# The last 64 rows of two batches on the two column halves of TensorE, and one product of batch 0 on row halves again

## The chip, the core and the metric

The kernel runs on one core of one Trainium2 chip. The metric is device time in microseconds (us), from start to end of one execution. A core has a matrix engine (TensorE, PE in the profile, with its weight loads listed apart as PEld), VectorE (DVE), ScalarE (ACT), GpSimd (POOL) and SyncE (SP, here it only issues transfers). TensorE multiplies a stationary block (the weights, lhsT) of up to 128 x 128 by a moving block of up to 512 columns and writes the result to PSUM, from where VectorE or ScalarE takes it. The stationary block can be smaller: the array can work as two column halves (128 x 64), two row halves (64 x 128) or four quarters (64 x 64), each with weights of its own.

## What is computed

A linear attention over 8 batches, 8 heads, 576 rows and 64 values per head, followed by an MLP mixer:

```python
def phi(x): return np.where(x > 0, x, np.exp(x) - 1.0) + 1.0
q_p, k_p = phi(q), phi(k)
kv  = einsum('bhsd,bhse->bhde', k_p, v);  z = sum(k_p, axis=2)
x   = einsum('bhsd,bhde->bhse', q_p, kv) / (einsum('bhsd,bhd->bhs', q_p, z) + 1e-6)
# x as (batch, 576, 512)
h   = relu(x^T @ w_tok1) @ w_tok2          # over the 576 rows, through 256
u   = x + h^T
out = u + relu(u @ w_ch1) @ w_ch2          # over the 512 columns, through 1536
```

The 576 rows of a batch are four blocks of 128 and a tail of 64. The product with `w_tok2` is called mm2 in the kernel.

## The kernel before

The batches are taken in pairs. While TensorE does the large products of batch n (mm3 and mm4, with `w_ch1` and `w_ch2`), small steps of batch n + 1 are put between them at fixed places (`AT`). R is 4, the number of full row blocks, so block R is the tail. D is 64, DM is 512, NT is 2 (256 = 2 x 128), T is 9.

mm2 takes a list of row blocks. For the tail it multiplies the full 128-column weights, of which 64 columns belong to the tail, and uses one half of the 128 rows that result: the lower half for an even batch, the upper for an odd one. The tails of a pair meet in one tile `ut` of 128 rows, which is transposed and gives one extra block of the large products.

```python
half = [slice(0, 64), slice(64, 128)]

def w2v(kt, r, b=0):
    at = D * (T * kt + 2 * r - (b if r == R else 0))
    return w2p[:, at:at + 128]

def mm2(n, rs, add=False):
    b = n % 2
    ...                                   # ps: two banks of PSUM from the pool "sm"
    for i, r in enumerate(rs):
        for kt in range(NT):
            nc.tensor.matmul(out=ps[:, i], lhsT=w2v(kt, r, b),          # L261
                             rhs=ar[b][:, kt, :], start=(kt == 0),
                             stop=(kt == NT - 1 and not add))
    ...
    if rs[0] == R:
        h = half[b]
        nc.vector.tensor_tensor(out=ut[n // 2 % 2][h], in0=ps[h, 0],    # L269
                                in1=x[b][h, R], op=ALU.add)
    ...
```

The steps of a batch n > 1, and where they stand in the order of the large products:

```python
out_ += [("mm2a", lambda: mm2(n, [0, 1])), ("mm2b", lambda: mm2(n, [2, 3])),
         ("mm2t", lambda: mm2(n, [R]))]
out_ += [("uta", lambda: utr_dma(n, [0, 1])), ("utb", lambda: utr_dma(n, [2, 3]))]
if n % 2:
    out_.append(("utt", lambda: utr_tail_dma(n // 2)))     # transposes ut by a transfer
...
AT = {"kv": 0, "nd00": 2, ..., "mm1": 9, "mm2a": 11, "mm2b": 12, "mm2t": 14,
      "uta": 11, "utb": 12, "utt": 14}
```

Batch 0 is done apart, at the start, where everything waits for the first loads. phi(k) is kept as two terms, kr and kp, both multiplied with v0. c is a group of four heads:

```python
def kv_first(c, copy):
    ps = sm_tile()[:, :, 0:2 * D]
    for k_ in (kr, kp):
        for t in range(T):
            on, off = k_ is kr and t == 0, k_ is kp and t == T - 1
            if k_ is kr:                                   # row halves, 64 x 128
                for a in range(2):
                    nc.tensor.matmul(out=ps[:, a], lhsT=k_[half[a], c, t],       # L366
                                     rhs=v0[half[a], 2 * c:2 * c + 2, t], start=on, stop=off)
            else:                                          # quarters, 64 x 64
                for a, i in QUARTERS:
                    nc.tensor.matmul(out=ps[half[i], a, i * D:(i + 1) * D],      # L371
                                     lhsT=k_[half[a], c, t, i],
                                     rhs=v0[half[a], 2 * c + i, t], start=on, stop=off)
    for i in range(2):
        copy(out=kvbd[0][half[i], c, :, i * D1:(i + 1) * D1 - 1],                # L375
             in_=ps[half[i], :, i * D:(i + 1) * D])
```

On row halves, the blocks of two different heads are multiplied with each other too; the copy takes only the two blocks that are wanted. Two products of batch 0 already stand on column halves (`ps[half[e]]`): L439, whose matmuls alternate between the halves, and L447, batch 0's own tail on one half.

```python
for kt in range(NT):                                       # in mm2_first, columns cs
    for e in range(2):
        nc.tensor.matmul(out=ps[half[e], i], lhsT=w2r[:, kt, :, 2 * r + e],      # L439
                         rhs=ar[0][:, kt, cs], start=(kt == 0), stop=(kt == NT - 1))
...
for kt in range(NT):                                       # in mm2_first_tail
    nc.tensor.matmul(out=ps[half[0]], lhsT=w2r[:, kt, :, 2 * R], rhs=ar[0][:, kt],   # L447
                     start=(kt == 0), stop=(kt == NT - 1))
```

Of the kernel before, what the change touches and what calls it, by code (L numbers as in the profile page):

```python
# [9 lines left out]
FP32 = mybir.dt.float32  # L10
BF16 = mybir.dt.bfloat16
AF = mybir.ActivationFunctionType
ALU = mybir.AluOpType
# [5 lines left out]
def kernel(  # L19
# [20 lines left out]
    nc = tc.nc  # L40

    B, H, S, D = q.shape
    DM = H * D
    DTOK = moe_w_tok1.shape[1]
    DCH = moe_w_ch1.shape[1]
    R = 4
    R1 = R + 1
    T = 2 * R + 1
# [3 lines left out]
    NT = DTOK // 128  # L52
# [10 lines left out]
    ps_sm = ctx.enter_context(tc.tile_pool(name="ps_sm", bufs=2, space=bass.MemoryType.PSUM))  # L63

    def const(name, shape, dt=BF16):
        return consts.tile(shape, dt, name=name, tag=name)
# [4 lines left out]
    w2p = const("w2p", [128, (NT * T + 1) * D])  # L71
# [6 lines left out]
    kr = const("kr", [128, 2, T, 2, D])  # L78
# [4 lines left out]
    x = [const(f"x{b}", [128, R1, DM]) for b in range(2)]  # L83
    ar = [const(f"ar{b}", [128, NT, DM]) for b in range(2)]
    u = [const(f"u{b}", [128, R, DM]) for b in range(2)]
    ut = [const(f"ut{i}", [128, DM]) for i in range(2)]
# [10 lines left out]
    half = [slice(0, 64), slice(64, 128)]  # L97
# [56 lines left out]
    def bank():  # L154
        return ps_big.tile([128, 512], FP32, name="bank", tag="big")
# [6 lines left out]
    def kv(n, cs):  # L162
        b = n % 2
        ps = ps_sm.tile([128, 2, 512], FP32, name="kv_ps", tag="sm")[:, :, 0:2 * D1].rearrange(
            "p a (c e) -> p a c e", c=2)
        for c in cs:
            for t in range(T):
                for a, i in QUARTERS:
                    nc.tensor.matmul(out=ps[half[i], a, c], lhsT=kp[half[a], c, t, i],  # L169
                                     rhs=vs[half[a], 2 * c + i, t],  # L170
                                     start=(t == 0), stop=(t == T - 1))
        cs = slice(cs[0], cs[-1] + 1)
        for i in range(2):
            at = slice(i * D1, (i + 1) * D1)
            nc.scalar.copy(out=kvbd[b][half[i], cs, :, at].transpose([0, 2, 1, 3]),
                           in_=ps[half[i], :, cs])
# [13 lines left out]
    def qtr(n, c, put=nc.scalar.copy):  # L190
        tp = ps_sm.tile([128, 2, 8, 128], BF16, name="tp", tag="sm")
        for h, ts in enumerate(TS):
            qtr_mm(c, ts, tp[:, h])
        for h, ts in enumerate(TS):
            qtr_put(n, c, ts, tp[:, h], put)
# [32 lines left out]
    def nd(n, g, rs):  # L228
        nd_mm(n, g, rs)
        nd_end(n, g, rs)  # L230
# [7 lines left out]
# [4 lines that stand above are left out]
    def mm1(n):  # L242
        b = n % 2
        ps = ps_sm.tile([128, NT, DM], FP32, name="a_ps", tag="sm")
        for mt in range(NT):
            ms = slice(128 * mt, 128 * mt + 128)
            for r in range(R1):
                nc.tensor.matmul(out=ps[:, mt], lhsT=w1t[:, b, ms] if r == R else w1[:, r, ms],  # L248
                                 rhs=x[b][:, r, :], start=(r == 0), stop=(r == R))
        for mt in range(NT):  # L250
            nc.scalar.activation(out=ar[b][:, mt, :], in_=ps[:, mt], func=AF.Relu)  # L251

    def mm2(n, rs, add=False):

        b = n % 2
        m = len(rs)
        ps = bank().rearrange("p (a d) -> p a d", a=1) if n == 1 else ps_sm.tile(
            [128, 2, DM], FP32, name="h_ps", tag="sm")
# [5 lines that stand above are left out]
            if add:  # L264
                nc.tensor.matmul(out=ps[:, i], lhsT=identity, rhs=x[b][:, r, :], start=False,
                                 stop=True)
        if rs[0] == R:
            h = half[b]
            nc.vector.tensor_tensor(out=ut[n // 2 % 2][h], in0=ps[h, 0], in1=x[b][h, R], op=ALU.add)  # L269
        elif add:  # L270
            nc.scalar.copy(out=u[b][:, rs[0]:rs[0] + m], in_=ps[:, 0:m])
        else:
            nc.vector.tensor_tensor(out=u[b][:, rs[0]:rs[0] + m], in0=ps[:, 0:m],  # L273
                                    in1=x[b][:, rs[0]:rs[0] + m], op=ALU.add)

    def mm2_half(n, c):
        b = n % 2
        cs = COLS[c]
        for rs in ([0, 1], [2, 3]):
            ps = ps_sm.tile([128, 2, 512], FP32, name="h_ps", tag="sm")[:, 0].rearrange(  # L280
                "p (r c) -> p r c", r=2)
            add = rs[0] == 0
            for i, r in enumerate(rs):
                if add:
                    nc.tensor.matmul(out=ps[:, i], lhsT=identity, rhs=x[b][:, r, cs],
                                     start=True, stop=False)
                for kt in range(NT):
                    nc.tensor.matmul(out=ps[:, i], lhsT=w2v(kt, r), rhs=ar[b][:, kt, cs],
                                     start=(kt == 0 and not add), stop=(kt == NT - 1))
            if add:  # L290
                nc.scalar.copy(out=u[b][:, 0:2, cs], in_=ps)
            else:
                nc.vector.tensor_tensor(out=u[b][:, 2:4, cs], in0=ps, in1=x[b][:, 2:4, cs],
                                        op=ALU.add)
# [22 lines left out]
    def sm_tile():  # L317
        return ps_sm.tile([128, 2, 512], FP32, name="bank2", tag="sm")
# [39 lines left out]
    def kv_first(c, copy):  # L358

        ps = sm_tile()[:, :, 0:2 * D]  # L360
        for k_ in (kr, kp):
            for t in range(T):
                on, off = k_ is kr and t == 0, k_ is kp and t == T - 1
                if k_ is kr:
                    for a in range(2):
                        nc.tensor.matmul(out=ps[:, a], lhsT=k_[half[a], c, t],  # L366
                                         rhs=v0[half[a], 2 * c:2 * c + 2, t],
                                         start=on, stop=off)
                else:
# [7 lines that stand above are left out]
# [95 lines left out]
    def utr_dma(n, rs):  # L472
        b = n % 2
        nc.sync.dma_start_transpose(
            out=uT[b][:, rs[0]:rs[0] + len(rs)].rearrange("p r j c -> p (r j) c"),
            in_=u[b][:, rs[0]:rs[0] + len(rs)].rearrange("p r d -> p (r d)"))

    def utr_tail_dma(p):
        nc.sync.dma_start_transpose(out=uTt, in_=ut[p % 2])
# [204 lines left out]
    def steps(n):  # L684

        out_ = [("kv", lambda: kv(n, range(2)))]
        if n == 1:
            puts = [nc.scalar.copy, nc.vector.tensor_copy if n == 1 else nc.scalar.copy]
            out_ += [(f"qt{c}", lambda c=c: qtr(n, c, puts[c])) for c in range(2)]
        for i, rs in enumerate(([0, 1], [2, 3], [4])):  # L690
            for g in range(2):
                out_.append((f"nd{i}{g}", lambda g=g, rs=rs: nd(n, g, rs)))
        out_.append(("mm1", lambda: mm1(n)))
        if n > 1:
            out_ += [("mm2a", lambda: mm2(n, [0, 1])), ("mm2b", lambda: mm2(n, [2, 3])),
                     ("mm2t", lambda: mm2(n, [R]))]
            out_ += [("uta", lambda: utr_dma(n, [0, 1])), ("utb", lambda: utr_dma(n, [2, 3]))]
            if n % 2:
                out_.append(("utt", lambda: utr_tail_dma(n // 2)))
        return out_  # L700
# [36 lines left out]
    for nm, fn in first[1:2] + late + first[2:3] + first[0:1] + first[3:]:  # L737
        fill += [(at0[nm], fn)]
    fill += [(23, fn) for fn in (
        lambda: mm4_end(0, 0), lambda: mm4_end(0, 1), lambda: mm2_half(1, 0),  # L740
        lambda: mm4_end(0, 2), lambda: mm2_half(1, 1), lambda: utr(1, [0]),
        lambda: mm2(1, [R]), lambda: utr(1, [1]), lambda: mm4_end(0, 3))]
    run(big, sorted(fill, key=lambda e: e[0]))
# [20 lines left out]
    for n in range(2, B):  # L764
        p, b = divmod(n, 2)
# [48 lines left out]
```

## Time and profile before

| | |
|---|---|
| device time, median of 3 | 264.82 us (264.30 to 264.83) |
| span of the profiled execution | 263.1 us |
| busy, TensorE | 253.5 us (96%) |
| busy, VectorE | 158.7 us (60%) |
| busy, ScalarE | 133.2 us (51%) |
| busy, GpSimd | 33.3 us (13%) |

In a line of a group or of the timeline, `L261 PE MATMUL h_ps<-ar,w2p 128*128 128x512 bf16 x2` is: line 261 of the kernel, the engine, the operation, the tile written and the tiles read, the part of the array used (128*128 is all of it, 128*64 a column half, 64*128 a row half, 64*64 a quarter), partitions and columns of the moving block, its type, and how many in a row. In a timeline the two numbers ahead are the start and the time from the first start to the last end, both in us; `[0.42 <-issue]` is the idle time of the engine just ahead and what ended it. In a list of waits the numbers are the sum in us, the count and the longest. Matmuls are pipelined, so the time that one holds the engine is read from the distance between starts. A timeline over a narrow window shows only the instructions that run in it, so its first start and count fix single matmuls.

### The profile page before, as it was taken

To read this page: it belongs to the slowest core of one execution; us is meant where nothing else is said; L and a number is where in the kernel's file an instruction comes from. 1 tells how busy PE (TensorE), PEld (TensorE's weight loads), DVE (VectorE), ACT (ScalarE), POOL (GpSimd) and SP (SyncE) were. 2 spreads that over 40 slices of the span, in tenths; PEclk is the share of its full clock that TensorE was granted. 3 is DMA by queue.
4 is the path that set the end of the run, shared out by engine and by line. 5 is a ranking of instruction groups with operands and counts; after the bars stand their busy time and mean duration, and the time that the engine had idled before them with its cause. 6 is when DMAs were issued, how large, how long until landed. Compare 5 with 4: busy or idle time off the path is not lost.

```text
span 263.1 us, 5193 instructions
## 1 busy us (share of the span) xinstructions
PE 253.5 (96%) x2118; PEld 134.1 (51%) x2136; DVE 158.7 (60%) x313; ACT 133.2 (51%) x204; POOL 33.3 (13%) x54
## 2 busy tenths in 40 slices
PE   7699999999999999999999999999999999999994
PEld 3485455554744554445554554455554454444642
DVE  5755978966839696939684287939684272420122
ACT  4664887368364458435780368335870353027300
POOL 9630210110002300020001300030001300000000
PEclk9999999999999999999999999999999999999999
DMA  7999999599306995699999990771074500730043
GB/s 256 246 204 278 370 205 397 190 205 401 151 0 130 192 367 223 140 272 393 288 360 197 283 397 14 157 165 33 0 134 119 120 2 0 152 107 2 0 99 103
DMA packets 50088, 48.35 MB, mean 184 GB/s; under 512 B 30288, under 2 KB 35536, under 8 KB 50064
## 3 DMA queue, kind: packets, MB, share of 16 engines
q1 hardware_dynamic: 41904, 35.53, 45.7%
q0 software_dynamic: 7440, 11.44, 20.7%
q10 hardware_dynamic: 720, 1.05, 1.3%
q8 instruction: 17, 0.28, 0.4%
q14 instruction: 7, 0.06, 0.1%
HBM read 35.85 MB, written 9.44 MB: 172 GB/s over the span
## 4 chain that ended last, share of the span: by engine, by line
PE 90%; DMA 3%; ACT 2%; DVE 1%; POOL 1%; issue 1%; ACTq 0%; POOLq 0%
PE h_ps L516 33%; PE c_ps L490 32%; PE a_ps L248 5%; PE h_ps L261 5%; PE c_ps L504 4%; PE nd_ps L210 3%; DMA cr<-in_v_dram 3%; PE kv_ps L169 2%; PE h_ps L553 1%; PE bank L428 1%; POOL qT L597 1%; PE bank L439 1%; PE bank L393 1%; PE bank L366 0%; DVE u L441 0%
## 5 line engine op out<-in xcount | busy, mean ns | idle before, releaser
L497 ACT ACTIVATE cr<-c_ps 128x512 bf16<-128x512 f32 x91 | 53.4, 599 | 76.3 <-PE c_ps L490 76.2
L490 PE MATMUL c_ps<-uT,wc 128*128 128x512 bf16 x384 | 91.5, 379 | 0.0
L516 PE MATMUL h_ps<-wc,cr 128*128 128x512 bf16 x365 | 84.5, 379 | 0.5
L516 PEld LDWEIGHTS <-cr 128*128 128x128 bf16 x372 | 36.0, 98 | 41.6
L490 PEld LDWEIGHTS <-wc 128*128 128x128 bf16 x384 | 35.7, 98 | 36.4 <-issue 0.9
L533 DVE TENSOR_TENSOR o_sb<-h_ps,u 128x512 f32<-128x512 f32 x31 | 21.1, 689 | 23.1 <-PE h_ps L516 21.4
L538 POOL DMA_DIRECT2D out_dram<-o_sb x24 | 15.0, 629 | 151.9 <-DVE o_sb L533 151.9
L222 DVE TENSOR_TENSOR x<-nd_ps,den 128x512 bf16<-128x512 f32 (+1 forms) x42 | 25.3, 603 | 1.4
L139 DVE TENSOR_SCALAR e<-e 128x1152 bf16<-128x1152 bf16 x30 | 13.9, 464 | 12.6 <-ACT e L125 12.6
L273 DVE TENSOR_TENSOR u<-h_ps,x 128x1024 bf16<-128x1024 f32 x12 | 14.3, 1220 | 10.1 <-PE h_ps L261 10.1
L125 ACT ACTIVATE e<-k_raw 128x1152 bf16<-128x1152 f32 x16 | 18.7, 1169 | 2.3 <-DMA k_raw<-in_k_dram 2.3
L125 ACT ACTIVATE e<-q_raw 128x1152 bf16<-128x1152 f32 x16 | 18.5, 1160 | 2.3 <-DMA q_raw<-in_q_dram 2.3
L219 DVE TENSOR_SCALAR den<-nd_ps 128x8 f32<-128x8 f32 (+1 forms) x42 | 6.9, 164 | 17.9 <-PE nd_ps L210 17.2
L210 PEld LDWEIGHTS <-qT 128*128 128x128 bf16 x140 | 11.4, 98 | 9.3 <-issue 0.2
L261 PE MATMUL h_ps<-ar,w2p 128*128 128x512 bf16 x58 | 15.6, 379 | 0.1
L210 PE MATMUL nd_ps<-kvbd,qT 128*128 128x130 bf16 x140 | 15.1, 223 | 0.0
L248 PE MATMUL a_ps<-x,w 128*128 128x512 bf16 x50 | 13.9, 379 | 0.3
L543 DVE TENSOR_TENSOR o_sb<-h_ps,ut 128x512 f32<-128x512 f32 x4 | 2.8, 690 | 18.7 <-PE h_ps L516 18.7
L251 ACT ACTIVATE ar<-a_ps 128x512 bf16<-128x512 f32 x14 | 7.6, 594 | 12.7 <-PE a_ps L248 12.7
L151 ACT CAST vs<-v_raw 128x1152 bf16<-128x1152 f32 x12 | 13.9, 1159 | 0.0
L140 DVE TENSOR_TENSOR qp<-e,y 128x1152 bf16<-128x1152 bf16 x16 | 12.1, 759 | 0.6
L131 DVE TENSOR_SCALAR y<-q_raw 128x1152 bf16<-128x1152 f32 x16 | 12.1, 757 | 0.3
(107 smaller groups left out, 220.9 us busy)
## 6 DMA issues: line engine op xcount, KB each, us to landing
k_raw<-in_k_dram SPq DMA_DIRECT2D x16, 576.0 KB, 9.7
q_raw<-in_q_dram SPq DMA_DIRECT2D x16, 576.0 KB, 7.0
v_raw<-in_v_dram SPq DMA_DIRECT2D x14, 576.0 KB, 11.2
out_dram<-o_sb POOLq DMA_DIRECT2D x24, 256.0 KB, 4.4
wc<-in_moe_w_ch_dram POOLq DMA_DIRECT2D x8, 384.0 KB, 9.7
out_dram<-o_sb SPq DMA_DIRECT2D x9, 128.0 KB, 2.3
out_dram<-o_sb ACTq DMA_DIRECT2D x7, 128.0 KB, 2.6
out_dram<-o_sb POOLq DMA_DIRECT2D x6, 128.0 KB, 6.8
```

Of the source, the lines that this page charges most:

```text
L125: nc.scalar.activation(out=e, in_=f, func=AF.Exp)
L139: nc.vector.tensor_scalar(out=e, in0=e, scalar1=1.0, scalar2=None, op0=ALU.min)
L210: nc.tensor.matmul(out=o[:, a], lhsT=qT[b][:, t0:t0 + 128], rhs=kvbd[b][:, c, a], start=True, stop=True)
L222: nc.vector.tensor_tensor(out=x[b][:, rs[0]:rs[0] + m, HG * D * g:HG * D * (g + 1)].rearrange("p r (h d) -> p r h d", h=HG), in0=v_[:, :, ...
L248: nc.tensor.matmul(out=ps[:, mt], lhsT=w1t[:, b, ms] if r == R else w1[:, r, ms], rhs=x[b][:, r, :], start=(r == 0), stop=(r == R))
L261: nc.tensor.matmul(out=ps[:, i], lhsT=w2v(kt, r, b), rhs=ar[b][:, kt, :], start=(kt == 0), stop=(kt == NT - 1 and not add))
L273: nc.vector.tensor_tensor(out=u[b][:, rs[0]:rs[0] + m], in0=ps[:, 0:m], in1=x[b][:, rs[0]:rs[0] + m], op=ALU.add)
L490: nc.tensor.matmul(out=ps, lhsT=wc1[:, kj, 128 * mc:128 * mc + 128], rhs=uT[b][:, :, kj], start=(kj == 0), stop=(kj == NDM - 1))
L497: nc.scalar.activation(out=cr[b][:, mc, :], in_=ps, func=AF.Relu)
L516: nc.tensor.matmul(out=ps, lhsT=crt[:, kc, :] if t == 8 else cr[b][:, kc, 128 * r:128 * r + 128], rhs=wc2[:, kc, :], start=(kc == 0), stop ...
L533: nc.vector.tensor_tensor(out=o, in0=ps, in1=u[b][:, r, :], op=ALU.add)
L538: (nc.scalar if last and e else put).dma_start(out=outv[2 * p + b, :, 2 * r0 + e:2 * r0 + e + 2 * m - 1:2], in_=live["o"][half[e], 0:m])
```

## The change

For pairs 1 to 3 (batches 2 to 7), the tail of the even batch is no longer computed in that batch's steps. In the odd batch's steps one function does both: each batch has 64-column weights on one column half of the array, and the two batches alternate, so that the halves can work at the same time on different data. The sum with x stays two additions on VectorE. Pair 0 is not touched. As for the start, the second term of kv for batch 0's first group (c = 0) goes from quarters to row halves, as its first term; the second group stays as it was.

```diff
+    def mm2_tails(p):
+        ps = ps_sm.tile([128, 2, DM], FP32, name="h_ps", tag="sm")[:, 0]
+        for kt in range(NT):
+            at = D * (T * kt + 2 * R)
+            for b in range(2):
+                nc.tensor.matmul(out=ps[half[b]], lhsT=w2p[:, at:at + D], rhs=ar[b][:, kt, :],
+                                 start=(kt == 0), stop=(kt == NT - 1))
+        for b in range(2):
+            h = half[b]
+            nc.vector.tensor_tensor(out=ut[p % 2][h], in0=ps[h], in1=x[b][h, R], op=ALU.add)
...
         for k_ in (kr, kp):
             for t in range(T):
                 on, off = k_ is kr and t == 0, k_ is kp and t == T - 1
-                if k_ is kr:
+                if c == 0 or k_ is kr:
                     for a in range(2):
...
         if n > 1:
-            out_ += [("mm2a", lambda: mm2(n, [0, 1])), ("mm2b", lambda: mm2(n, [2, 3])),
-                     ("mm2t", lambda: mm2(n, [R]))]
+            out_ += [("mm2a", lambda: mm2(n, [0, 1])), ("mm2b", lambda: mm2(n, [2, 3]))]
+            if n % 2:
+                out_.append(("mm2t", lambda: mm2_tails(n // 2)))
```

## The prediction

> **What bounds the kernel now.** I read the page from the top. Its slices ask which engine is never idle:
>
> ```profile
> PE   7699999999999999999999999999999999999994
> DVE  5755978966839696939684287939684272420122
> PEclk9999999999999999999999999999999999999999
> ```
>
> TensorE is full from slice 3 to 39 at full clock; VectorE is not. The chain of work that ended last agrees:
>
> ```profile
> PE 90%; DMA 3%; ACT 2%; DVE 1%; POOL 1%; issue 1%; ACTq 0%; POOLq 0%
> ```
>
> The list of what TensorE waited for (sum in us, count, longest) says where it is not alone; three more waits, of 0.2 us each, end the list:
>
> ```profile
> PE bank L577 <- DVE ones L590: 1.5, 1, 1.5
> PE bank L366 <- DMA cr<-in_v_dram: 1.2, 1, 1.2
> PE bank L180 <- DVE qp L140: 0.8, 1, 0.8
> PE bank L393 <- ACT kvbd L375: 0.3, 1, 0.3
> ```
>
> All waits are in the start or the first pair; the longest are before 12 us. From batch 2 on TensorE waits for nobody that the profile shows. So a matmul taken out of pairs 1 to 3 moves the end by its own length, and so does one put into the first 25 us after the v data has come.
>
> How long one matmul holds TensorE is not its listed duration (379 ns for 512 columns, which overlaps the next one), but the distance from one start to the next. The timeline of TensorE around the tail of batch 5 (165 us):
>
> ```profile
> 164.77 0.81 PE L516 MATMUL h_ps<-wc,cr 128*128 128x512 bf16 x3
> 165.42 0.59 PE L261 MATMUL h_ps<-ar,w2p 128*128 128x512 bf16 x2
> 165.85 1.03 PE L516 MATMUL h_ps<-wc,cr 128*128 128x512 bf16 x4
> ```
>
> The two L261 matmuls are the tail of one batch: 165.85 - 165.42 = 0.43 us, 0.215 us each, with nothing lost before or after. The tail of batch 4 (133.21 to 133.64, one record missing) also takes 0.43.
>
> **What it costs to change the shape of the array.** The kernel already has a product on column halves: the tail of batch 0 (L447, two matmuls on one half). The timelines of TensorE and of its weight loads there:
>
> ```profile
> 24.73 0.81 PE L490 MATMUL c_ps<-uT,wc 128*128 128x512 bf16 x3
> 25.47 0.70 PE L447 MATMUL bank<-ar,w 128*64 128x512 bf16 x2
> 26.11 0.82 PE L490 MATMUL c_ps<-uT,wc 128*128 128x512 bf16 x3
> ```
>
> ```profile
> 25.47 0.31 PEld L447 LDWEIGHTS <-w 128*64 128x64 bf16 x2 [0.42 <-issue]
> 26.10 0.55 PEld L490 LDWEIGHTS <-wc 128*128 128x128 bf16 x4 [0.33 <-issue]
> ```
>
> Narrow windows put the last L490 before them at 25.16; its 512 columns are through at 25.16 + 0.215 = 25.375. L447 starts only at 25.47 (0.10 later), and its weight load starts at the same instant: it could not be drawn ahead under the full-array matmul. Its second matmul starts at 25.79, 0.32 and not 0.215 after the first, so another 0.105 is the exposed first load. It is through at 26.00, and the full-array matmuls resume at 26.11, 0.11 later. One visit costs 0.10 + 0.105 + 0.11 = 0.315 us whatever is done in it.
>
> Two halves do run together. L439 alternates halves as the new code will; three narrow windows show its last six matmuls:
>
> ```profile
> 20.06 0.53 PE L439 MATMUL bank<-ar,w 128*64 128x256 bf16 x6
> 20.18 0.41 PE L439 MATMUL bank<-ar,w 128*64 128x256 bf16 x4
> 20.29 0.30 PE L439 MATMUL bank<-ar,w 128*64 128x256 bf16 x2
> ```
>
> The count falls by two at each step and the starts are 0.115 us apart: a pair of 256 columns takes 0.115, where the full-array L428 of 256 columns started every 0.105 (18.27, 18.38, 18.48). A pair costs about one full matmul plus 0.01. The first pair of L439, after the full-array L428 (through at 18.81), started at 18.91 and the second at 19.13: the same 0.10 and the same extra 0.105.
>
> [...] the trace has 202 ns for a 128x64 load against 98 ns for a 128x128 one. [...]
>
> **The change part by part.** Part A, the tails. Removed: for batches 2 to 7, two full matmuls each, 12 x 0.215 = 2.58 us. Added: for pairs 1 to 3, two pairs of half-array matmuls of 512 columns each. Per pair of batches: 0.10 to drain, 0.105 for the exposed load, 2 x (0.215 + 0.01) = 0.45, 0.11 back: 0.765 us, against 4 x 0.215 = 0.86 before. Saving 0.095 per pair of batches, three times 0.29 us. Without the mode change it would have been 3 x 0.41 = 1.23; three quarters of the arithmetic gain go into going to column mode and back. All of it lies on TensorE, so on the path.
>
> VectorE does the same two 64x512 additions per pair of batches (L269, 688 ns), now back to back. The transfer of the transposed tail must wait for the second, 0.69 us more. In the pass from 147 us the tail was ready at 167.03 and its transfer was issued only at 169.84, behind the transposes of q; its first use is L504 at 189.16. Hidden. PSUM: one buffer fewer is taken in even batches. ar and x of the even batch are held until the tail of the odd one; they are rewritten in the next pass. I see no new wait.
>
> Part B, batch 0's first group. The kp term goes from quarters (36 matmuls of 64x64) back to row halves (18 of 64x128). The timeline of the start gives both:
>
> ```profile
> 11.25 0.68 PE L366 MATMUL bank<-cr,kr 64*128 64x128 bf16 x18 [1.16 <-DMA cr<-in_v_dram]
> 11.86 0.48 PE L371 MATMUL bank<-cr,kp 64*64 64x64 bf16 x36
> 12.27 0.68 PE L180 MATMUL bank<-identity,qp 128*128 128x128 bf16 x9
> ```
>
> L366 runs in pairs every 0.055 us (narrow windows: 11.25, 11.30, 11.36, 11.41, 11.47), so nine pairs take 0.50, and 0.61 passes to L371: 0.11 is again a mode change. L371 takes 0.41 to L180, of which 0.11 is the change to the full array and 0.30 the nine quartets. New: kr and kp both on row halves, no change between them, 0.50 + 0.11 = 0.61 for kp in place of 0.11 + 0.30 + 0.11 = 0.52. Part B costs 0.09 us. kv_first(0) is followed on TensorE by dense work (L180, L386, L393, L352, then the second group at 14.15), so the delay passes on; the copy to kvbd ends at 12.94 and L393 starts at 13.05, and both move alike.
>
> Sum: -0.29 + 0.09 = -0.20 us; 264.82 - 0.20 = 264.6 us.
>
> **Rivals.** (1) The mode change is hidden in the steady passes, because the queue of full-array work is deep there: then A saves up to 1.23 us, net -1.1, 263.7 us. Against it: L447 stood in dense L490 work, and paid. (2) The halves do not overlap at 512 columns, because loads of 202 ns for both halves come one after the other and cannot hide under 215 ns: then each pair of batches takes 0.86 + 0.315, A costs 0.95 us, and the time is 265.9. Against it: L439 overlaps at 256 columns, where hiding is harder. (3) A new wait: the later transposed tail or the additions back to back hold up VectorE's freeing of PSUM for mm4. The DVE row has idle slices and mm4 has four banks, some 2 us ahead; it would add 0.5 us per pair at most, 266. (4) B's cost is swallowed by a later wait of the start (L457 waits 0.2 us for VectorE at 21.05): then -0.29 alone, 264.5. VectorE's work there follows TensorE too, so I expect not.
>
> **Range and chances.** The three times of before span 264.30 to 264.83, more than the effect that I expect. Rival 1 in part gives the low end, a dearer mode change (0.45 instead of 0.315) with run-to-run scatter the high end: 263.9 to 265.2. 2% is 5.3 us; all the matmuls touched together are 2.6 us of TensorE, so neither side can reach it: 0.005, 0.99, 0.005.
>
> **What would show it.** Around each new tail: a first half-array start 0.10 us after the last full matmul is through, a second pair 0.32 us after the first, full work again some 0.77 us after the first gap began; TensorE's busy time about unchanged, with no new wait in its list. In the start, L180 at 12.36 and not 12.27, with no 64x64 form in the first group. Wrong, if the four half matmuls span 0.45 us in all (rival 1), if four starts 0.2 us apart appear (rival 2), or if TensorE shows a wait on VectorE or on a transfer after 60 us (rival 3).

## The result and the profile after

The changed kernel takes 263.62 us (median of 6 runs, 263.54 to 264.36) beside 264.82 us before: ratio 0.9960, 95% interval 0.9946 to 0.9974, so 0.7 to 1.4 us less. The prediction was 264.6 us, 0.2 us less, with 263.9 as the low end of its range. The direction is right; the gain is several times the one predicted.

From the page of the changed kernel, the slices and the shares of the chain:

```profile
PE   7699999999999999999999999999999999999993
...
PE 90%; DMA 3%; ACT 2%; DVE 1%; POOL 1%; issue 1%; ACTq 0%; POOLq 0%
```

And what TensorE waited for (the first four):

```profile
PE bank L589 <- DVE ones L602: 1.5, 1, 1.5
PE bank L378 <- DMA cr<-in_v_dram: 1.4, 1, 1.4
PE bank L180 <- DVE qp L140: 1.1, 1, 1.1
PE bank L405 <- ACT kvbd L387: 0.3, 1, 0.3
```

Nothing new is waited for; TensorE still sets the end. (Lines 276 and later have moved by 12: L516 is L528 now, L366 is L378, L428 is L440.) So the gain must lie in how long TensorE's own work lasts. The timeline around the first new tail:

```profile
104.89 1.89 PE L528 MATMUL h_ps<-wc,cr 128*128 128x512 bf16 x8
...
106.70 0.14 PEld L282 LDWEIGHTS <-w2p 128*64 128x64 bf16 x4 [0.42 <-issue]
106.71 0.62 PE L282 MATMUL h_ps<-ar,w2p 128*64 128x512 bf16 x4
107.26 1.84 PEld L528 LDWEIGHTS <-cr 128*128 128x128 bf16 x10 [0.41 <-issue]
107.26 2.12 PE L528 MATMUL h_ps<-wc,cr 128*128 128x512 bf16 x9
```

Two narrow windows give the last full matmul ahead and the second pair:

```profile
106.40 0.38 PE L528 MATMUL h_ps<-wc,cr 128*128 128x512 bf16 x1
```

```profile
106.95 0.38 PE L282 MATMUL h_ps<-ar,w2p 128*64 128x512 bf16 x2
```

The last full matmul is through at 106.40 + 0.215 = 106.615. The halves start 0.10 us later, the second pair 0.24 us after the first, and full work resumes at 107.26, about 0.10 after the second pair is through. The visit takes 107.26 - 106.615 = 0.645 us, and the next full matmul comes 0.23 rather than 0.215 us later: 0.66. Predicted were 0.765. All four weight loads are issued within 0.03 us of one another and last 108 ns each; the prediction had 202.

The start, in the timeline of the changed kernel:

```profile
11.47 0.68 PE L378 MATMUL bank<-cr,kr 64*128 64x128 bf16 x18 [1.42 <-DMA cr<-in_v_dram]
...
11.97 0.68 PE L378 MATMUL bank<-cr,kp 64*128 64x128 bf16 x18
...
12.58 0.68 PE L180 MATMUL bank<-identity,qp 128*128 128x128 bf16 x9
```

L180 follows 1.11 us after the first of these, against 1.02 before: the predicted 0.09. But a few microseconds later time comes back. In the chain, the 20 matmuls of batch 0's mm1 (L428 before, L440 now) hold 2.18 us where they held 2.35; the first line is from before, the second from the changed kernel:

```profile
16.62 2.35 PE bank L428 x20
16.94 2.18 PE bank L440 x20
```

That is the second thing that the prediction did not have.

**Where v lands is scatter, so the path is counted from there.** In each trace but e5's, TensorE starts its first matmul with v when the transfer of v has landed, between 10.28 and 11.47 us in the traces below. Here "path" is the span less that start; it takes this scatter out of a single profile, up to the 0.05 us to which a span is rounded. "mm1" is what the chain gives to the 20 matmuls just named; 2.18 is their undisturbed length.

| kernel | time, us | ratio to before, interval | span - start = path, us | mm1, us |
|---|---|---|---|---|
| before | 264.82 | 1 | 263.1 - 11.25 = 251.85 | 2.35 |
| e9 before, again | 264.69 | 1.0003 (0.9985 to 1.0020) | 263.1 - 10.99 = 252.11 | 2.64 |
| changed | 263.62 | 0.9960 (0.9946 to 0.9974) | 262.6 - 11.47 = 251.13 | 2.18 |
| e1 changed, again | 263.75 | 0.9968 (0.9954 to 0.9982) | 261.9 - 10.88 = 251.02 | 2.18 |
| e2 tails only | 264.31 | 0.9973 (0.9957 to 0.9990) | 261.6 - 10.34 = 251.26 | 2.49 |
| e3 row halves only | 264.66 | 0.9986 (0.9968 to 1.0004) | 262.4 - 10.59 = 251.81 | 2.18 |
| e4 tails, strided weights | 264.04 | 0.9972 (0.9958 to 0.9987) | 262.4 - 11.10 = 251.30 | 2.18 |
| e5 changed + 18 tiny | 264.55 | 0.9991 (0.9974 to 1.0009) | 261.7 - 10.66 = 251.04 | 2.18 |
| e6 tails in turn | 263.61 | 0.9954 (0.9939 to 0.9969) | 261.4 - 10.28 = 251.12 | 2.18 |
| e7 all pairs | 263.74 | 0.9964 (0.9943 to 0.9985) | 262.1 - 11.34 = 250.76 | 2.18 |
| e8 contiguous first products | 263.55 | 0.9959 (0.9942 to 0.9976) | 261.8 - 10.99 = 250.81 | 2.18 |
| e10 before + 18 tiny | 267.65 | 1.0111 (1.0078 to 1.0144) | 264.5 - 11.18 = 253.32 | 2.18 |
| e11 all pairs, late transposes | 263.90 | 0.9976 (0.9961 to 0.9991) | 262.1 - 11.13 = 250.97 | 2.18 |
| e12 all pairs, late additions | 263.42 | 0.9951 (0.9931 to 0.9971) | 261.7 - 11.27 = 250.43 | 2.18 |

### The profile page after: what moved, and what is told of

Its sections match the earlier page's. It is cut to its first block, busy times and chain, and to the rows that moved or that the text cites. A ratio compares the mean times of both kernels' runs of the same rounds, so it can differ in the third digit from the quotient of the medians.

```text
span 262.6 us, 5152 instructions
## 1 busy us (share of the span) xinstructions
PE 252.5 (96%) x2100; PEld 133.0 (51%) x2118; DVE 158.8 (60%) x313; ACT 133.2 (51%) x204; POOL 33.4 (13%) x54
## 4 chain that ended last, share of the span: by engine, by line
PE 90%; DMA 3%; ACT 2%; DVE 1%; POOL 1%; issue 1%; ACTq 0%; POOLq 0%
PE h_ps L528 33%; PE c_ps L502 32%; PE a_ps L248 5%; PE c_ps L516 4%; PE h_ps L261 4%; PE nd_ps L210 3%; DMA cr<-in_v_dram 3%; PE kv_ps L169 2%; PE h_ps L565 1%; PE bank L440 1%; POOL qT L609 1%; PE bank L378 1%; PE h_ps L282 1%; PE bank L451 1%; PE bank L405 1%
## 5 line engine op out<-in xcount | busy, mean ns | idle before, releaser
L502 PE MATMUL c_ps<-uT,wc 128*128 128x512 bf16 x384 | 91.5, 379 | 0.0
L528 PE MATMUL h_ps<-wc,cr 128*128 128x512 bf16 x363 | 84.3, 379 | 0.5
L528 PEld LDWEIGHTS <-cr 128*128 128x128 bf16 x372 | 35.6, 98 | 41.6 <-issue 1.2
L502 PEld LDWEIGHTS <-wc 128*128 128x128 bf16 x384 | 35.6, 98 | 36.5 <-issue 0.9
L139 DVE TENSOR_SCALAR e<-e 128x1152 bf16<-128x1152 bf16 x30 | 14.1, 469 | 15.6 <-ACT e L125 15.5
L261 PE MATMUL h_ps<-ar,w2p 128*128 128x512 bf16 x48 | 12.5, 379 | 0.1
```

What stands on the lines that cost most here:

```text
L139: nc.vector.tensor_scalar(out=e, in0=e, scalar1=1.0, scalar2=None, op0=ALU.min)
L261: nc.tensor.matmul(out=ps[:, i], lhsT=w2v(kt, r, b), rhs=ar[b][:, kt, :], start=(kt == 0), stop=(kt == NT - 1 and not add))
L502: nc.tensor.matmul(out=ps, lhsT=wc1[:, kj, 128 * mc:128 * mc + 128], rhs=uT[b][:, :, kj], start=(kj == 0), stop=(kj == NDM - 1))
L528: nc.tensor.matmul(out=ps, lhsT=crt[:, kc, :] if t == 8 else cr[b][:, kc, 128 * r:128 * r + 128], rhs=wc2[:, kc, :], start=(kc == 0), stop ...
```

## The experiments

The theories: (1) the first traces are typical and the tails save 0.2 us per pair of batches; (2) they are not; (3) the unexplained part sits in part B; (4) it is a stop of TensorE at a fixed count of its instructions; (5) it is a stop for another reason.

**e1: the changed kernel again.** No edit.

> The changed kernel once more, for a second profile and to see what of the 1.2 us repeats. Theory 1 (the traces of before and after are typical: each pair of batches saves 0.2 us, part B costs 0.09): 0.5 us under the kernel before, ratio 0.998. Theory 2 (the first profile fell on a run whose v loads came late; the tails or part B save more than it shows): 1.2 us under it, ratio 0.9955, and a second profile with a span near 261.9 us that shows where the other 0.7 us are.

Ratio 0.9968, about 0.85 us less. Its path is 251.02 us, with the first profile's 251.13 a mean of 251.08; the two of before have 251.98. The difference of paths is 0.90 us, inside both intervals. By the timed runs neither theory is singled out: 0.9968 lies between 0.998 and 0.9955, and the interval holds both. The spans alone (262.6 and 263.1 in the first two profiles) had shown 0.5, because v landed 0.22 us later in the changed kernel's.

**e2: part A alone.**

```diff
-                if c == 0 or k_ is kr:
+                if k_ is kr:
```

> Part A alone: the tails on column halves, the first group's second term still on quarters. Theory 1: 0.6 us under the kernel before, 0.1 under the changed kernel. Theory 3 (part B is where the unexplained gain sits): 0.6 us under the kernel before, and 0.6 us above the changed kernel. Theory 2 with the gain in the tails: 1.2 to 1.3 us under the kernel before.

0.3% less, 0.5 to 0.7 us by its ratio and its median: what theory 1 has for the tails. But the path, 251.26, lies 0.2 us above the changed kernel's, where theory 1 had it 0.1 below; mm1 lasts 2.49 us here, 0.31 more than 2.18. The device times of this run exceed their spans by 1.9 us in the median and up to 2.6 in single runs, against 1.77 in nearly all others (also in e5, by 1.87 and up to 3.1); no reason for that was found, so spans are compared: their median is 262.4 us, beside 262.0 for e1 and 263.0 for the kernel before in the same measurement.

**e3: part B alone.** The kernel before with `c == 0 or` in that line.

> Part B alone: the first group's second term on row halves, the tails as before. Theory 1: TensorE's next work starts 1.11 us after the first of these matmuls in place of 1.02, and the time is 0 to 0.1 us above the kernel before. Theory 3: 0.6 us under the kernel before, with the v loads landing earlier or a wait in the start gone.

The ratio's interval reaches 1. The trace has both terms: L366's 36 matmuls take 1.18 us in the chain where L366 and L371 took 0.68 + 0.41 = 1.09, and mm1 takes 2.18 again. So the local cost is 0.09 us and the stop is gone. The path, 251.81, is 0.17 below the mean of before.

**e4: the stride of the weights.**

```diff
-                nc.tensor.matmul(out=ps[half[b]], lhsT=w2p[:, at:at + D], rhs=ar[b][:, kt, :],
+                nc.tensor.matmul(out=ps[half[b]], lhsT=w2r[:, kt, :, 2 * R], rhs=ar[b][:, kt, :],
```

> The changed kernel, but the 64 columns of weights of the tails are read from the tile in which they lie 9 elements apart, not from the one in which they are contiguous. The prediction took the slow weight load (202 ns, 0.105 us of it exposed) as a price of the column mode; the changed kernel's loads took 108 ns. If the stride is the cause: loads near 200 ns, a second pair some 0.32 us after the first and not 0.24, and 0.08 to 0.1 us more per pair of batches, 0.3 us in all. If not: loads of 108 ns and the changed kernel's time.

One line of its trace by source, and its timeline at the first tail:

```profile
L281 PEld LDWEIGHTS <-w x12: 189/200/216, 106.3 to 224.0; 128*64 128x64 bf16 x12
```

```profile
106.34 0.71 PE L281 MATMUL h_ps<-ar,w 128*64 128x512 bf16 x4
106.98 1.41 PEld L527 LDWEIGHTS <-cr 128*128 128x128 bf16 x8 [0.33 <-issue]
```

The same four products with the same shape: loads of 200 ns (minimum, median, maximum in the first line), and the halves hold TensorE for 106.98 - 106.34 = 0.64 us instead of 107.26 - 106.71 = 0.55. The path is 0.22 us longer than in the changed kernel (3 x 0.09 = 0.27 expected). The stride of 9 elements makes the load slow, not the column mode, in which both these 200 ns and the 108 ns of the changed kernel were measured; e8 repeats this within one tile.

**The two parts, cut apart in the traces.** Two starts that the timelines list separate part B from the tails: the first matmul of kv of batch 2 (L169, near 62 us), after part B and ahead of the tails of pairs 1 to 3, and the first matmul of the last product (L553 before), after them.

| trace | first matmul with v to kv of batch 2, us | from there to the last product, us |
|---|---|---|
| before | 62.43 - 11.25 = 51.18 | 256.35 - 62.43 = 193.92 |
| e9 before, again | 62.44 - 10.99 = 51.45 | 256.37 - 62.44 = 193.93 |
| e3 row halves only | 61.69 - 10.59 = 51.10 | 255.70 - 61.69 = 194.01 |
| e2 tails only | 61.65 - 10.34 = 51.31 | 254.92 - 61.65 = 193.27 |
| changed | 62.56 - 11.47 = 51.09 | 255.83 - 62.56 = 193.27 |
| e1 changed, again | 61.98 - 10.88 = 51.10 | 255.25 - 61.98 = 193.27 |
| e4 strided weights | 62.20 - 11.10 = 51.10 | 255.73 - 62.20 = 193.53 |

So the tails are worth 0.65 us, whether part B is there or not, and the stride takes back 0.26 of it, as expected. Part B is worth 0.08, 0.36 and 0.21 us beside before, e9 and e2, as the stop in mm1 is short or long.

**e5: 18 tiny matmuls in the changed kernel.**

```diff
     warm(1, 256)
+    fillps = bank()
+    for _ in range(18):
+        nc.tensor.matmul(out=fillps[:, 0:2], lhsT=identity, rhs=ones, start=True, stop=True)
     kv_first(0, act)
```

> The changed kernel plus 18 tiny matmuls (128x128 weights, 2 columns) while TensorE waits for the v loads: 36 more TensorE instructions, as many as part B takes away, and no work on the path as long as v lands later. Without part B, the traces show TensorE stopping between the first and the second matmul of the second half of mm1 for 0.17 to 0.31 us, though all that it reads is ready; with part B this gap is gone. Theory 4 (the gap sits at a fixed count of TensorE instructions, and part B moves that count to later work): the gap comes back at the same matmul, 0.17 to 0.31 us, and the time rises by as much. Theory 5 (part B removes it by its longer time or its other shape): no gap, and the changed kernel's time.

The gap does not come back in the profile: mm1 2.18 us, path 251.04. By itself this spoke against theory 4. In this trace, however, the matmul in question is due only at 17.17 us (17.06 + 0.107), and in e2 the stop had ended at 17.05. So the run could not tell. Nor were the tiny matmuls off the path here: TensorE's list has no wait for v, and the chain runs through them until 10.73 us.

**e6: both matmuls of a half one after the other.**

```diff
-        for kt in range(NT):
-            at = D * (T * kt + 2 * R)
-            for b in range(2):
+        for b in range(2):
+            for kt in range(NT):
+                at = D * (T * kt + 2 * R)
```

> The changed kernel with the four tail matmuls in the order batch 0, batch 0, batch 1, batch 1, so that both matmuls of one half follow one another. If the gain needs the halves to alternate: at least the middle two may still overlap, so three steps of 0.215 in place of two, 0.2 us or more per pair of batches, 0.65 us in all. If overlap is decided without regard to order: the changed kernel's time. If there was no overlap anyway: the same time too, but with four starts 0.2 us apart.

```profile
105.51 0.63 PE L282 MATMUL h_ps<-ar,w2p 128*64 128x512 bf16 x4
106.06 2.49 PEld L528 LDWEIGHTS <-cr 128*128 128x128 bf16 x13 [0.41 <-issue]
```

The visit is the same 0.55 us from first start to full work, and narrow windows show two matmuls running by 105.52 and four started by 105.76, as with alternation. Path and ratio are the changed kernel's. At this length of four matmuls the order did not matter.

**e7: pair 0 too.** `mm2_tails(0)` in place of `mm2(1, [R])`, on a bank of the other pool; `mm2_first_tail` is taken out.

> The changed kernel with pair 0 done in the same way: batch 0's tail leaves the large products at 25 us (0.735 us there, with strided weights on one half) and joins batch 1's tail (0.43 us). By the changed kernel's own visits (0.645 us from the last full matmul being through to the next full one): 0.735 + 0.43 - 0.66 = 0.5 us less, about 263.2 us, if the later second addition on VectorE (done some 1.4 us after the matmuls) does not hold up the transpose of the tail, 1.6 us after them.

The time is the changed kernel's, within the intervals; the path is 0.3 us shorter, not 0.5. In the chain, 0.04 us of issue at 54.72 follow the second addition to ut (54.02 + 0.71): TensorE had to wait for VectorE, where the addition of batch 0 now stands ahead of batch 1's. Its six L502 matmuls there take 1.73 us from first start to last end, where six took 1.46 in the changed kernel: 0.27 us of the 0.5 is lost there.

**e8: contiguous weights in batch 0's mm2.** These are other columns of w_tok2, so batch 0's result is another one.

```diff
-                    nc.tensor.matmul(out=ps[half[e], i], lhsT=w2r[:, kt, :, 2 * r + e],
+                    nc.tensor.matmul(out=ps[half[e], i], lhsT=w2[:, kt, D * (2 * r + e):D * (2 * r + e + 1)],
...
-            nc.tensor.matmul(out=ps[half[0]], lhsT=w2r[:, kt, :, 2 * R], rhs=ar[0][:, kt],
+            nc.tensor.matmul(out=ps[half[0]], lhsT=w2[:, kt, 0:D], rhs=ar[0][:, kt],
```

> The changed kernel with contiguous 64-column weights in batch 0's mm2 (other columns of w_tok2 than the right ones, so batch 0's u is another). If the stride is what makes the loads slow: loads of 108 in place of 202 ns for the first products and the tail of batch 0; the second matmul of batch 0's tail 0.24 and not 0.32 us after the first; pairs of 256 columns every 0.107 and not 0.115 us; in all up to 0.35 us less, part of it lost to waits for VectorE at 20 us. If the column mode itself makes first loads slow: no change.

The path is 0.27 us shorter than the changed kernel's. The trace by source of the first products:

```profile
L451 PEld LDWEIGHTS <-w x32: 106/110/110, 18.6 to 21.3; 128*64 128x64 bf16 x32
```

They had 189/204/214 in the changed kernel, from the same tile. The first 24 matmuls take 1.50 us and not 1.68, and batch 0's tail 0.55 us to the next full matmul and not 0.64. This is the second place where the load's price goes with the stride.

**e9: the kernel before again.** No edit.

> The kernel before once more, for a second profile of it: ratio 1.000. Counted from the first matmul that takes v (which starts when the v loads land, at another time in each execution) to the end of the span, the first profile has 251.85 us, the two profiles of the changed kernel 251.13 and 251.02. If these differences are the change: 251.7 to 252.0 here, and the unexplained gap in the second half of mm1 (0.17 us, between the first and second of its matmuls) is there again. If the gap was chance: no gap.

The gap is there again, longer. The chain of e9:

```profile
16.36 1.20 PE bank L428 x11
17.56 0.28 issue
17.84 1.16 PE bank L428 x9
```

It stops after the eleventh of the 20 matmuls, as in the two other traces without part B. Between that matmul and the next there is no semaphore wait in the program. The path came out at 252.11, above what was expected, by that longer gap.

**e10: the 18 tiny matmuls in the kernel before.** The edit of e5.

> The kernel before plus the 18 tiny matmuls while TensorE waits for v. Theory 4 (TensorE stops at a fixed count of its instructions until something arrives some 6.6 us after v): the stop moves 36 instructions earlier, to the second group's products with kvbd, where TensorE arrives some 2 us sooner, so it becomes 1 us or more and the time rises by as much. Theory 5 (nothing to do with the count): the gap stays at the second matmul of the second half of mm1, or is not there, and the time is that of the kernel before.

```profile
15.81 0.33 PE bank L393 x3
16.14 1.58 issue
17.72 0.56 PE bank L393 x7
```

The stop has moved to after the third product of the second group, exactly 36 instructions (18 loads and 18 matmuls) earlier in the program, and it ends at nearly the same time, 17.72 us here, 17.82 and 17.84 in the two traces of before (17.05 in e2). It is 1.58 us long in the trace. The time rises by 1.1%, which is more than that; but four of the six runs had a granted clock of 0.984 to 0.994, and the two at clock 1.0 have spans of 264.3 and 264.5 us, 1.5 to 1.7 above the median of 262.8 of the kernel before beside them. Counted in weight loads, matmuls and semaphore instructions (which only wait for another engine), all four traces stop after 448: 223 loads, 223 matmuls and 2 semaphore instructions in before, e9 and e2; 224, 223 and 1 here. Theory 4 stands: at this instruction TensorE stopped until 17.05 to 17.84 us. In the changed kernel the 448th is the ninth matmul of L451, which runs at 19.0 to 19.6 us in its two traces, and no stop shows there.

**e11 and e12: repairs of e7.** e11 moves the transposes of pair 0's tail behind the second large product:

```diff
-    utr_tail(0)
+    fill += [(1, lambda: utr_tail(0))]
```

> All four pairs with the tails together, and the transposes of pair 0's tail moved behind the next large product, since in the run with all pairs TensorE stopped some 0.2 us ahead of them for the second addition on VectorE. By the trace of that run: 0.2 us less than it, 0.5 us less than the changed kernel, about 263.2 us; TensorE's path from the first matmul that takes v to the end near 250.5 us.

No gain: in the chain TensorE goes on at 54.57 us, right after the second addition has ended (54.53), all the same, and it stops again at 60.33 us for an eviction of mm3 on ScalarE. So it was not the transposes that waited for the addition, or not they alone. e12 takes the additions of pair 0 out of `mm2_tails` and puts them last on VectorE, and the transposes behind the eighth product:

```diff
-            nc.vector.tensor_tensor(out=ut[p % 2][h], in0=ps[h], in1=x[b][h, R], op=ALU.add)
+        live["tails"] = ps                  # the additions go into mm2_tails_add
+        if p:
+            mm2_tails_add(p)
...
-        lambda: mm2_tails(0), lambda: utr(1, [1]), lambda: mm4_end(0, 3))]
+        lambda: mm2_tails(0), lambda: utr(1, [1]), lambda: mm4_end(0, 3),
+        lambda: mm2_tails_add(0))]
...
-    fill += [(1, lambda: utr_tail(0))]
+    fill += [(7, lambda: utr_tail(0))]
```

> All four pairs with the tails together; pair 0's two additions go behind the last eviction of mm4 on VectorE, and the transposes of its tail behind the eighth large product. In the run before, TensorE lost some 0.2 us at 54.57 us waiting for VectorE and 0.2 us at 60.33 us waiting for ScalarE, and a further 0.1 us. If these waits were what ate the 0.5 us that pair 0 should give: no such stop between 53 and 61 us, TensorE's path from the first matmul that takes v to the end 250.5 us (251.1 in the changed kernel), and 263.2 us. If something else ate it: the path stays near 251.0 us and the time near 263.8.

```profile
52.61 0.55 PE bank L282 x4
53.16 0.55 PE tp L322 x8
53.72 7.00 PE c_ps L508 x32
```

No stop between 53 and 61 us in the chain, and a path of 250.43 us, 0.65 shorter than the changed kernel's. The ratio to before is 0.9951 (0.9931 to 0.9971). It is the shortest path of all these runs that keep the whole computation; by the timed runs alone its lead on the changed kernel (263.42 beside 263.62 and 263.75) is not clear of their scatter.

## Why the prediction was wrong

**Right.** TensorE's own work is the bound, before and after (90% of the chain in both), and no new wait came in. The halves overlap: two pairs 0.24 us apart, four matmuls in 0.55 us. The gap ahead of the halves is 0.10 us and the one on the way back 0.10; what TensorE does in them the traces do not say. The local price of part B is 0.09 us. VectorE's two additions back to back and the later transfer of the tail are hidden: in the pass with the tail at 165 us the additions end at 167.07, the transfer is issued at 169.38, and its first use is at 188.80.

**Wrong in size: "another 0.105 is the exposed first load".** The working took L447 and L439 as the model of a visit. Both read weights 9 elements apart; the new code reads the contiguous copy w2p, which the diff shows. Measured, the second pair comes 0.24 and not 0.32 us after the first, so 0.025 and not 0.105 us of the load is exposed, and no extra 0.01 per pair shows. A visit costs 0.66 and not 0.765 us. Against 0.86 before, that is 0.20 per pair of batches, 0.6 in all. The stretch that holds the three tails is 0.65 us shorter, where the prediction had 0.29; the last 0.05 were not traced to a place.

The prediction also took 202 against 98 ns as a price of the column mode, which the trace of before did not show: those two loads differ in stride as well as in shape. With contiguous weights, a 128x64 load takes 108 ns (L282), beside 98 for a 128x128 load of the full array (L528); the other 94 ns came with the stride, as e4's 200 ns for the same product show.

**Wrong in sign: "Part B costs 0.09 us ... so the delay passes on".** It does pass on, but part B also takes 36 instructions out of TensorE's stream, and so the stop after instruction 448 disappears. It had cost 0.17 and 0.46 us in the two traces of before (2.35 and 2.64 against 2.18), 0.31 in the mean. Part B is thus worth 0.31 - 0.09 = 0.22 us in the mean, not -0.09. Nothing in the change aimed at this: that part of the gain was luck. The stop stands in the profile of before, in the list of what the weight loads waited for; the prediction's list did not show it, because it asked for matmuls only:

```profile
PEld L428 <- issue: 0.3, 1, 0.3
```

**The sum.** 0.65 from the tails and 0.22 from part B make 0.87 us. The paths differ by 0.90, the two timed comparisons by 1.1 and 0.85 us by their ratios, with 0.87 inside both intervals. Rival 1, a hidden mode change with a net gain of 1.1 us, would fit the first time alone, but the trace contradicts it: the gaps of 0.10 us are there.

**What the stop waits for, and what stays open.** The packed trace holds every packet of the DMA queues with its start and length. The page of before lists a queue q8 of the kind "instruction", with 17 packets and 0.28 MB. In the trace of before, the window from 15.4 to 15.5 us has the first of them:

```profile
q8 instruction: 1, 0.02, 60.9%
```

60.9% of 16 engines' 0.1 us is its length, 0.97 us; it runs from 15.46 to 16.44. The stop ends at 17.82, 1.38 us after it. In e9 this packet is through at 16.47 and the stop ends at 17.84, in e2 at 15.68 and 17.05, in e10 at 16.44 and 17.72: 1.28 to 1.38 us each time. In the ten traces without a stop, the packet had been through for 1.4 to 2.5 us when the load after the 448th instruction started. The least is e5's, 15.65 to 17.06, 1.41 us, just more than in the four with a stop; so the missing gap there does not speak against theory 4. The end of the stop goes with this packet in the four traces that have one. That it waits for the packet is inferred from these times alone: a trace does not say what a packet holds, nor for which engine. Why it comes no earlier, what takes the 1.3 to 1.4 us after it, and what lowered the clock in e10 are not shown.

## What to carry to other kernels

When you take a cost from another place of the same kernel, compare the access pattern of the operand as well as its shape: here the stride of the weights, not the mode of the array, made a first load cost 0.08 us more per visit. A visit to the column halves paid a gap of 0.10 us on each side, so it needs enough columns: with 4 x 512 columns it gained 0.2 us of 0.86. And look at the idle time of the weight loads that ends with "issue" early in a program, and at the packets of the instruction queue ahead of it; here 36 instructions fewer ahead of it took away a stop of 0.17 to 0.46 us, against 0.09 us that the exchange of matmuls itself cost, and 36 more made the stop 1.58 us.

## What the runs showed of the hardware that was not expected

A stop of TensorE at a fixed count of its instructions (after the 448th here), ending between 17.05 and 17.84 us and 1.28 to 1.38 us after the first packet of the instruction queue is through, at a weight load of mm1 in three traces and of L393 in e10: 0.17 to 0.46 us as written, 1.58 us with 36 instructions more ahead of it, none with 36 fewer. A 128x64 weight load takes 108 ns when its columns are contiguous and 200 to 204 ns when they are 9 elements apart. Four half-array matmuls of 512 columns on two halves take 0.55 us to the next full matmul, alternating or in turn.
